# Second-stage scores over all 128 rows of the matmul array, fed by copies of their operands, with the second-stage products moved behind the first stage's

## The chip, the cores and the metric

The kernel runs on one core of a Trainium2 chip. The metric is the device time of one execution in microseconds (us); smaller is better. The engines are named as the profile names them: PE (matmuls; PEld is its weight load), DVE, ACT and POOL (work on rows of elements), SP (here it only issues DMA transfers). Each engine runs its own instructions strictly in the order in which they were built, and waits where an operand or a buffer isn't there yet.

## The reference

Two attentions follow each other. The first has 8 batches of 8 heads over 576 positions of width 64, and keeps only scores within tau of their row's maximum. Its output, heads side by side, is x of the second, which has four experts with causal attention; each row takes the two experts with the highest gate.

```python
scores = scale * np.matmul(q, k.transpose(0, 1, 3, 2))
thresh = np.max(scores, axis=-1, keepdims=True) - tau
scores = np.where(scores >= thresh, scores, -1000000000.0)
attn = softmax(scores); x = heads_side_by_side(np.matmul(attn, v))
...
for e in range(E):                      # E = 4 experts of width 64
    q = x @ wq[e]; k = x @ wk[e]; v = x @ wv[e]
    scores = scale * (q @ k.transpose(0, 2, 1))
    scores = np.where(causal, -1000000000.0, scores)
    ye = softmax(scores) @ v @ wo[e]
    out += (gate weight of e, zero unless e is in the top 2) * ye
```

## The kernel before

**Tiles and stages.** The 576 positions are four row tiles of 128 and a rest of 64 (`R = 4`, tile number 4 is the rest, for both heads at once). Heads are taken in pairs: pair `n` of 32, four pairs to a batch. The main loop has one step per row tile of a pair (`i = 5n + s`, tiles in the order `TS`). A step scores a tile (`scores`: PE into PSUM bank pairs, DVE maximum, ACT exponential, DVE threshold, POOL normalization), transposes the tile of two steps ago (`transp`, PE and ACT), prepares the next pair's q and k (`prep`), and at steps 1 and 4 of a pair multiplies transposed tiles by the values (`attnv`).

**Precision.** Operands of the scores are split into a rounded high part and a rest. In the first stage DMA copies inside SBUF (`spread`, queue of SP) lay high part and rest of q above each other, 64 rows each, so that a head needs two products over 128 rows. In the second stage, before the change, a head needs three products over 64 rows (high times high, high times rest, rest times high: `HHL`); expert 0 of an expert pair lies in rows 0 to 63 and expert 1 in rows 64 to 127, so their products alternate between the two halves of the array.

**The second stage** runs one batch behind the first. For batch `b` and expert pair `ep` (0 or 1), which together are called a key here, there are projections (`project`, PSUM tiles `pj`), values and gates (`values`, `v2`), scores (`scores2`, `s2`, over `w = 128 (t + 1)` columns for row tile `t`, then a causal mask added by a bf16 product), transposes (`transp2`, `t2`), products with the values (`attnv2`, `av2`) and at the end `output` (`o`). In the profile the digit of a name is dropped, so `s2` reads `s`, `t2` reads `t`, `av2<-pt2,v2` reads `av<-pt,v`.

**Order.** A plan in Python writes the program: `pe[1]` is the plan's own clock for PE, `fill` puts second-stage pieces into a step until the step's share is used, `tiled` is called at steps 1 to 4 of a pair and puts in up to two due value products and one score tile, and `AFTER_...` are the waits that the plan leaves between a piece and its follower. `pr` gives every instruction a priority, by which a scheduler then sets each engine's order. Second-stage PSUM tiles come from four banks (`ps_g`) that transposes, projections and value products share; a full score tile takes two of them, one per expert.

**Array shapes.** The profile writes rows*columns of the array in use: 128*128 for most products, 128*64 for products with values (`av`), and 64*128 for the second-stage scores of row tiles 0 to 3.

Of the kernel before, what the change touches and what calls it, by code (L numbers as in the profile page):

```python
# [28 lines left out]
AFTER_S2, AFTER_V, AFTER_T2, AFTER_AV2 = 7000, 8500, 1800, 2000  # L29
BETWEEN_S2, AFTER_V_END = 2000, 5000  # L30

# [7 lines left out]
CUT = 2  # L39
T_END = (2, 3, 4, 1, 0)  # L40
T_MID = (4, 3, 2, 1, 0)
# [7 lines left out]
    "max": -0.509, "thr": -0.091, "exp": 0.327, "stt": -2.461, "sum": -1.419, "nrm": 0.098,  # L49
# [6 lines left out]
PPB = 4  # L56
P2B = 3
PTB = 9
PTTB = 4
VB = 3  # L60
E_PTT = "A"
# [3 lines left out]
def kernel(  # L65
# [112 lines left out]
    def load_pair(n):  # L178
        b, hp = divmod(n, NPAIR)
        hs = slice(2 * hp, 2 * hp + 2)  # L180
        vm = one.tile([P, 2, R, D], F32, tag="vm", name=f"vm_{n}", bufs=VB)
        pr("ld")
        def load(dst, src):
            r = nc.sync.dma_start(dst, src)
            if n in (1, 2):
                tc.add_manual_dep(r.ins, SPREAD[0].name, NOSYNC, reason="order")
        for t, x in ((km, k), (qm, q)):
            load(t[:, :, :R], x[b, hs, :SM, :].rearrange("h (p r) d -> p h r d", r=R))
            load(t[:ST, :, R], x[b, hs, SM:, :].rearrange("h s d -> s h d"))
        load(vm, v[b, hs, :SM, :].rearrange("h (p r) d -> p h r d", r=R))  # L190
        for j, rows in enumerate((slice(0, ST), slice(ST, P))):
            load(vtz[n % VB][rows, j], v[b, 2 * hp + j, SM:, :])
        VS[n] = (vm, vtz[n % VB])

# [246 lines left out]

    q2ds = [zeros(f"q2d{i}") for i in range(2)]
    Q2, V2, GW, GT = {}, {}, {}, {}

    def project(b, ep, cs):

        first, last = cs[0] == 0, cs[-1] == NC - 1
        for i, (wh, wl) in enumerate(((wqh, wql), (wkh, wkl))):
            if last:
                Q2[b, ep, i] = one.tile([P, 2, S], F32R, tag=f"q2{ep}{i}", name=f"q2_{b}_{ep}_{i}")  # L450
            t = Q2.get((b, ep, i))
# [88 lines left out]
    def scores2(b, t, ep):  # L540
        q2, k2 = Q2[b, ep, 0], Q2[b, ep, 1]
        nmx = small.tile([P, 2], F32, tag="nmx", name=f"nm2_{b}_{ep}_{t}")
        sm = small.tile([P, 2], F32, tag="sm", name=f"sm_{b}_{ep}_{t}")
        pr("s2")
        if t < R:
            w = (t + 1) * P
            if b == B - 1:
                g = ps_s.tile([P, 2, 512], F32, tag="s", name=f"s2_{b}_{t}_{ep}")
                gg = [g[:, j] for j in range(2)]
            else:  # L550
                gg = [gbank(f"s2_{b}_{t}_{ep}_{j}") for j in range(2)]
            for i, (x, y) in enumerate(HHL):
                for j in range(2):
                    sl = slice(j * D, (j + 1) * D)
                    matmul(gg[j][:, :w], q2[sl, x, t * P:w], k2[sl, y, :w], start=(i == 0), stop=False)
            for j in range(2):
                matmul(gg[j][:, t * P:w], ident_b, mask, start=False, stop=True)
            views = [g[:, :w] for g in gg]
        else:
            w = S  # L560
            g = ps_s.tile([P, 2, 512], F32, tag="s", name=f"s2_{b}_{t}_{ep}")
            for hf in range(2):
                cols = slice(hf * HS, (hf + 1) * HS)
                for i, (x, y) in enumerate(HHL):
                    matmul(g[:, hf, :HS], q2ds[ep][:, x], k2[:, y, cols],
                                     start=(i == 0), stop=(hf == 0 and i == 2))
# [108 lines left out]
    def project_some():  # L675

        while proj:
            b, what, g = proj[0]
            if what == "v" and left.get(b - 1, 0) or any(x[1] == b - 1 and what == f"q{x[3]}" for x in S2):
                return False  # L680
            try:
# [4 lines left out]
                if what[0] == "q":  # L686
                    S2.extend((0, b, t, int(what[1])) for t in (T_MID if b < B - 1 else T_END))
                elif what == "v":
# [3 lines left out]
        return False  # L692

    def score_tile():
        _, b, t, ep = S2.pop(0)
        scores2(b, t, ep)
        if b in GW and not unscaled:
            scale2(b, t, ep)
# [13 lines left out]
    def transposable():  # L712
        return due(T2) and len(unscaled) < len(T2) and len(A2) < 2

# [18 lines left out]

    def tiled():

        for _ in range(2):
            if due(A2):
                value_tile()
        if S2 and S2[0][2] < R and len(T2) < P2B:
            score_tile()  # L740
# [10 lines left out]
    for _ in prep(0):  # L751
        pass
    load_pair(1)
    pre = iter(())
    goal = 0.0
    for i in range(N + 2):
# [24 lines left out]
        if slot:  # L781
            m, at = (n, 4) if s == 4 else (n - 1, 6)
            if 0 <= m < NPR:
                attnv(m, TS[slice(*AV_AT[at])])
                if at == 6 and m % NPAIR == NPAIR - 1:
                    begin(m // NPAIR)
            tiled()
        else:
            next(tr, None)
            if s in MORE:  # L790
                tiled()
        for _ in sc:
# [8 lines left out]
        fill(goal)  # L801
        if S2 and S2[0][2] == R and len(T2) < P2B:
            score_tile()
# [3 lines left out]
    while proj or S2 or T2 or A2 or O2:  # L807
# [7 lines left out]
        elif transposable():  # L815
            transpose_tile()
        elif S2 and len(T2) < (P2B if S2[0][1] < B - 1 else PPB) and pe[1] >= since:
            score_tile()
# [33 lines left out]
```

## Time and profile before

| | |
|---|---|
| device time, median of 3 runs | 1035.93 us (1033.07 to 1035.97) |
| profiled execution: own time | 1033.38 us |
| profiled execution: span from first to last instruction | 1031.7 us |
| PE, DVE, ACT, POOL busy, share of the span | 94%, 79%, 63%, 40% |
| granted PE clock, mean | 0.99 |

The span is 1.7 us shorter than the execution's own time. A busy share counts the modelled time of instructions. In a timeline, the distance from the start of one matmul to the start of the next is what a matmul costs PE in a dense stream; the duration beside it is its whole passage and overlaps with the next.

### The profile page before, as it was taken

What the parts mean: (1) busy time and instruction counts of PE and PEld (TensorE: products, weight loads), DVE (VectorE), ACT (ScalarE), POOL (GpSimd) and SP (SyncE); (2) the same over time, 40 slices, a digit from 0 to 9 for tenths busy, and PEclk for the clock granted to TensorE, in tenths of its full rate; (3) what the DMA queues carried; (4) which work ended last, traced back from release to release, by engine and by line L of the source; (5) the groups of instructions that cost most, each with busy time, mean ns of one, the idle gap of its engine ahead of it and who ended that gap; (6) DMA issues with size and microseconds to landing.
All of it is one profiled execution on the core that took longest, in us unless ns stands there. A gap on an engine that the chain in (4) does not pass through costs nothing.

```text
span 1031.7 us, 26572 instructions
## 1 busy us (share of the span) xinstructions
PE 966.5 (94%) x9520; PEld 863.5 (84%) x9520; DVE 816.5 (79%) x2374; ACT 651.6 (63%) x1564; POOL 408.4 (40%) x700
## 2 busy tenths in 40 slices
PE   4778999999999999999999999999999999999998
PEld 3676898789888898888987898978988889888975
DVE  4778688877888779888789878887788877988564
ACT  3667566765667656765667656676566765676554
POOL 2556424533244334443344332453324533433122
PEclk9998999999999999999999999999999999999999
DMA  6555423344223443225343242334322344311101
GB/s 156 142 128 141 121 73 91 102 117 119 59 72 95 133 112 93 61 68 143 90 103 94 72 124 75 91 102 126 110 56 73 96 132 112 79 30 44 42 2 46
DMA packets 83891, 96.11 MB, mean 93 GB/s; under 512 B 29745, under 2 KB 54321, under 8 KB 83761
## 3 DMA queue, kind: packets, MB, share of 16 engines
q1 hardware_dynamic: 83296, 93.83, 34.5%
q8 instruction: 76, 1.25, 0.5%
q10 hardware_dynamic: 464, 0.59, 0.2%
q14 instruction: 55, 0.44, 0.1%
HBM read 30.42 MB, written 9.44 MB: 39 GB/s over the span
## 4 chain that ended last, share of the span: by engine, by line
PE 59%; DVE 17%; ACT 13%; issue 5%; POOL 4%; DMA 1%; SPq 0%; DVEq 0%; ACTq 0%; POOLq 0%
PE av L159 18%; PE s L159 13%; PE tm L162 8%; PE pj L159 7%; DVE pp L356 5%; PE v L159 4%; PE o L159 4%; ACT p L575 3%; ACT pp L354 3%; PE t L162 3%; DVE nmx L349 3%; DVE x L439 2%; ACT pt L144 2%; PE qkT L162 2%; POOL pp L364 2%
## 5 line engine op out<-in xcount | busy, mean ns | idle before, releaser
L364 POOL TENSOR_SCALAR pp<-pp,ss 128x576 f32<-128x576 f32 x288 | 212.8, 750 | 408.4 <-DVE ss L370 313.0
L356 DVE SCALAR_TENSOR_TENSOR pp<-s,thr,pp 128x576 f32<-128x576 f32 x288 | 233.0, 814 | 77.3 <-ACT pp L354 72.5
L354 ACT ACTIVATE pp<-s,nmx 128x576 f32<-128x576 f32 x288 | 213.7, 746 | 80.6 <-DVE nmx L349 76.8
L349 DVE TENSOR_REDUCE nmx<-s 128x1 f32<-128x576 f32 x288 | 215.8, 751 | 41.6 <-PE s L159 40.4
L159 PE MATMUL s<-kt,qt 128*128 128x288 f32 x1024 | 205.3, 319 | 5.8 <-DMA qt<-hl 5.4
L162 PE MATMUL tm<-ident,pp 128*128 128x128 f32 x1152 | 166.2, 278 | 22.1 <-POOL pp L364 15.8
L159 PE MATMUL av<-pt,vm 128*64 128x128 f32 (+1 forms) x2560 | 167.8, 267 | 0.0
L159 PEld LDWEIGHTS s<-kt,qt 128*128 128x128 f32 x1024 | 151.9, 194 | 15.5 <-DMA qt<-hl 5.7
L162 PEld LDWEIGHTS tm<-ident,pp 128*128 128x128 f32 x1152 | 136.1, 143 | 33.2 <-POOL pp L364 22.6
L159 PEld LDWEIGHTS av<-pt,vm 128*64 128x64 f32 x2560 | 140.0, 138 | 15.4 <-issue 11.4
L144 ACT COPY pt<-tm 128x512 f32<-128x512 f32 x199 | 113.6, 589 | 58.6 <-PE tm L162 56.3
L575 ACT ACTIVATE p<-s,nm 128x384 f32<-128x384 f32 (+3 forms) x144 | 78.9, 551 | 63.4 <-DVE nm L573 59.0
L589 POOL TENSOR_SCALAR p<-p,sm,gw 128x512 f32<-128x512 f32 (+3 forms) x128 | 77.1, 610 | 81.4 <-ACT pt L144 35.4
L140 ACT ACTIVATE x<-av 128x256 fp32r<-128x256 f32 (+1 forms) x96 | 48.0, 500 | 71.5 <-PE av L159 49.6
L573 DVE TENSOR_REDUCE nm<-s 128x1 f32<-128x384 f32 (+3 forms) x144 | 71.1, 513 | 24.2 <-PE s L159 21.4
L162 PE MATMUL t<-ident,p 128*128 128x128 f32 x384 | 61.1, 284 | 15.9 <-DVE ss L369 8.9
L159 PE MATMUL av<-ptt,vtz 128*64 128x128 f32 (+1 forms) x640 | 68.8, 263 | 0.0
L140 ACT ACTIVATE pt<-t 128x512 f32<-128x512 f32 (+2 forms) x112 | 57.9, 541 | 15.6 <-PE t L162 14.2
L159 PE MATMUL v<-wvh,x 128*128 128x260 f32 x320 | 64.8, 287 | 0.0
L162 PEld LDWEIGHTS t<-ident,p 128*128 128x128 f32 x384 | 43.0, 144 | 25.9 <-POOL p L589 14.3
L439 DVE TENSOR_TENSOR x<-av,x 128x256 fp32r<-128x256 f32 (+1 forms) x96 | 47.6, 495 | 19.2 <-ACT x L140 16.0
L159 PE MATMUL av<-pt,v 128*64 128x128 f32 (+1 forms) x896 | 57.9, 262 | 1.9 <-ACT p L575 1.2
(132 smaller groups left out, 1808.9 us busy)
## 6 DMA issues: line engine op xcount, KB each, us to landing
kt<-hl SPq DMA_DIRECT2D x252, 144.0 KB, 2.7
qt<-hl SPq DMA_DIRECT2D x128, 128.0 KB, 2.4
km<-in_k_dram SPq DMA_DIRECT2D x32, 256.0 KB, 3.0
qm<-in_q_dram SPq DMA_DIRECT2D x32, 256.0 KB, 3.2
vm<-in_v_dram SPq DMA_DIRECT2D x32, 256.0 KB, 2.8
out_dram<-ob SPq DMA_DIRECT2D x32, 256.0 KB, 2.4
km<-in_k_dram SPq DMA_DIRECT2D x32, 32.0 KB, 2.7
qm<-in_q_dram SPq DMA_DIRECT2D x32, 32.0 KB, 2.7
```

The source lines that it names most:

```text
L140: nc.scalar.activation(dst, src, AF.Copy)
L144: nc.any.tensor_copy(dst, src)
L159: queued(nc.tensor.matmul(out, x, y, **kw), x, ns if x.shape[0] == P else ns / 2)
L162: queued(nc.tensor.transpose(out, x, ident), x, 109)
L349: nc.vector.tensor_reduce(nmx[:, js], sv, axis=AX.XY, op=ALU.max, negate=True)
L354: nc.scalar.activation(e, sv, AF.Exp, bias=nmx[:, js])
L356: nc.vector.scalar_tensor_tensor(e, sv, thr[:, js], e, op0=ALU.is_ge, op1=ALU.mult, accum_out=ss[:, js])
L364: nc.gpsimd.tensor_scalar(p, p, ss[:, h:h + 1], 0.0, op0=ALU.mult, op1=ALU.add)
L439: nc.vector.tensor_tensor(xl, gs, xh.bitcast(F32), op=ALU.subtract)
L573: nc.vector.tensor_reduce(nmx[:, j:j + 1], sv, axis=AX.X if t < R else AX.XY, op=ALU.max, negate=True)
L575: nc.scalar.activation(p2[:, j * SM:j * SM + w] if t < R else halves(p2[:, :S]), sv, AF.Exp, bias=nmx[:, j:j + 1], accum_out=sm[:, j:j + 1])
L589: nc.gpsimd.tensor_scalar(p, p, sm[:, j:j + 1], gg[:, j:j + 1], op0=ALU.mult, op1=ALU.mult)
```

## The change

It has four parts. The second-stage score operands are copied into two new tiles (`q2x`, `k2x`) by twelve DMA copies on SP's queue per key (`spread2`), as the first stage does it, and an expert's scores are two products over 128 rows in place of three over 64; the row tile of the rest stays as it was. Score tiles of up to 256 columns hold both experts in one PSUM bank. Due value products of the second stage are put in only at steps 1 and 4, directly behind the first stage's (up to three), and no longer at steps 2 and 3; up to three transposed tiles may wait for them, where it was two. Buffers follow: one pair of `q2` tiles for both expert pairs where there were two, two value buffers (`VB`) where there were three, their loads behind `attnv`, and for the last batch the order `T_END` begins with tile 4.

```diff
-BETWEEN_S2, AFTER_V_END = 2000, 5000
+BETWEEN_S2, AFTER_V_END, AFTER_SPREAD = 2000, 5000, 6000
-T_END = (2, 3, 4, 1, 0)
+T_END = (4, 2, 3, 1, 0)
-VB = 3
+VB = 2
...
+    def spread2(b, ep):
+        qs, ks = Q2[b, ep, 0], Q2[b, ep, 1]
+        heads = [slice(j * D, (j + 1) * D) for j in range(2)]
+        q2x, k2x = X2 if (b, ep) != (B - 1, EP - 1) else (
+            two.tile([P, 2, SM], F32R, tag="qt", name="q2x_end"),
+            two.tile([P, 2, 2, S], F32R, tag="kt", name="k2x_end")[:, :, :, :SM])
+        Q2[b, ep] = (q2x, k2x)
+        pr("dm2")
+        for j, sl in enumerate(heads):
+            for x, rows in enumerate(heads):
+                for dst, src in ((q2x[rows, j], qs[sl, x, :SM]), (k2x[heads[0], j, x], ks[sl, x, :SM]),
+                                 (k2x[heads[1], j, x], ks[sl, x, :SM])):
+                    nc.sync.dma_start(dst.bitcast(F32), src.bitcast(F32))
...
-                gg = [gbank(f"s2_{b}_{t}_{ep}_{j}") for j in range(2)]
-            for i, (x, y) in enumerate(HHL):
-                for j in range(2):
-                    sl = slice(j * D, (j + 1) * D)
-                    matmul(gg[j][:, :w], q2[sl, x, t * P:w], k2[sl, y, :w], start=(i == 0), stop=False)
+                g = gbank(f"s2_{b}_{t}_{ep}_0")
+                gg = [g, g[:, w:] if 2 * w <= 512 else gbank(f"s2_{b}_{t}_{ep}_1")]
             for j in range(2):
+                for i in range(2):
+                    matmul(gg[j][:, :w], q2x[:, j, t * P:w], k2x[:, j, i, :w], start=(i == 0), stop=False)
                 matmul(gg[j][:, t * P:w], ident_b, mask, start=False, stop=True)
...
-        return due(T2) and len(unscaled) < len(T2) and len(A2) < 2
+        return due(T2) and len(unscaled) < len(T2) and len(A2) < 3
...
-    def tiled():
-        for _ in range(2):
+    def tiled(most):
+        for _ in range(most):
             if due(A2):
                 value_tile()
-        if S2 and S2[0][2] < R and len(T2) < P2B:
+        if scorable(False) and len(T2) < P2B:
             score_tile()
...
-            tiled()
+            tiled(3)
         else:
             next(tr, None)
             if s in MORE:
-                tiled()
+                tiled(0)
```

The built order shows three places. The first is a score tile of 256 columns on PE, in the second stage of batch 3 (`s2_3_1_1` is row tile 1 of its expert pair 1), with the row ahead of it; before:

```order
L159 MATMUL av2_3_4_1_8700<-pt2t_3_1_8610,v2_3_7530 64x64 x2
L159 MATMUL s2_3_1_1_0_8715<-q2_3_1_1_8035,q2_3_1_0_7970 128x256 x3
L159 MATMUL s2_3_1_1_1_8716<-q2_3_1_1_8035,q2_3_1_0_7970 128x256 x3
L159 LDWEIGHTS ident_b_78
L159 MATMUL s2_3_1_1_0_8715<-mask_80,ident_b_78 128x128
L159 LDWEIGHTS ident_b_78
L159 MATMUL s2_3_1_1_1_8716<-mask_80,ident_b_78 128x128
L159 MATMUL s_19_4_0_8746<-hl_19_8279,qd1_116 128x288 x6
```

Now, the same score tile:

```order
L159 MATMUL s_19_1_1_8863<-kt_19_8190,qt_19_8189 128x288 x3
L159 MATMUL s2_3_1_1_0_8924<-k2x_123,q2x_122 128x256 x2
L159 LDWEIGHTS ident_b_78
L159 MATMUL s2_3_1_1_0_8924<-mask_80,ident_b_78 128x128
L159 MATMUL s2_3_1_1_0_8924<-k2x_123,q2x_122 128x256 x2
L159 LDWEIGHTS ident_b_78
L159 MATMUL s2_3_1_1_0_8924<-mask_80,ident_b_78 128x128
L162 MATMUL t2_3_3_1_0_8940<-ident_73,p2_3_3_1_8671 128x128 x4
```

Six products into two PSUM tiles became four into one, each expert's mask follows its own products, and the rows ahead of it and behind it now use the whole array, as it does itself.

The second place is a value product of the same batch on PE (`av2_3_1_0`); before it stands alone at a step 3, between transposes and a score tile:

```order
L162 MATMUL tm_18_0_1_8560<-ident_73,pp_18_0_8298 128x128 x4
L162 MATMUL tt_18_0_8567<-ident_73,pp_18_0_8298 128x128
L159 MATMUL av2_3_1_0_8573<-pt2_3_1_0_0_8449,v2_3_7530 64x128 x4
L159 MATMUL s2_3_2_1_0_8582<-q2_3_1_1_8035,q2_3_1_0_7970 128x384 x3
L159 MATMUL s2_3_2_1_1_8583<-q2_3_1_1_8035,q2_3_1_0_7970 128x384 x3
```

Now value products stand behind the first stage's, and the next score tile behind them (`av_18_2` is the first stage's):

```order
L159 MATMUL av_18_2_8792<-ptt_18_3_8760,vtz0_100 64x128 x2
L159 MATMUL av2_3_0_0_8821<-pt2_3_0_0_0_8728,v2_3_7670 64x128 x2
L159 MATMUL av2_3_4_1_8826<-pt2_3_4_1_0_8774,v2_3_7670 64x64 x8
L159 MATMUL av2_3_4_1_8826<-pt2t_3_1_8778,v2_3_7670 64x64 x2
L159 MATMUL s2_3_2_1_0_8841<-k2x_123,q2x_122 128x384 x2
```

Rows of one array shape were moved together: over the whole program PE's order before changes its array shape 328 times from one matmul to the next, and 192 times now.

The third place is SP's queue where the copies of batch 3's expert pair 1 fall, behind the last copies for pair 19; before:

```order
L282 DMA qt_19_8280<-hl_19_8279 64x512 x4
L184 DMA km_97<-in_k_dram 64x2x64
L184 DMA qm_96<-in_q_dram 128x2x256
L184 DMA qm_96<-in_q_dram 64x2x64
L657 DMA out_0_dram<-ob_3_4_8779 64x512
```

Now:

```order
L290 DMA qt_19_8189<-hl_19_8188 64x512 x4
L468 DMA q2x_122<-q2_3_1_0_8077 64x512
L468 DMA k2x_123<-q2_3_1_1_8342 64x512 x2
L468 DMA q2x_122<-q2_3_1_0_8077 64x512
L468 DMA k2x_123<-q2_3_1_1_8342 64x512 x2
L468 DMA q2x_122<-q2_3_1_0_8077 64x512
L468 DMA k2x_123<-q2_3_1_1_8342 64x512 x2
L468 DMA q2x_122<-q2_3_1_0_8077 64x512
L468 DMA k2x_123<-q2_3_1_1_8342 64x512 x2
L183 DMA km_97<-in_k_dram 64x2x64
L183 DMA qm_96<-in_q_dram 128x2x256
```

Twelve copies stand ahead of the loads for the next pair; the first six serve expert 0, the other six expert 1, and the first of each six waits for PE's last product from the tiles that it overwrites.

## Rows read from the trace of the kernel before

**Rows 1.** The page: busy time of PE and DVE, and the chain by engine.

```profile
PE 966.5 (94%) x9520; PEld 863.5 (84%) x9520; DVE 816.5 (79%) x2374; ACT 651.6 (63%) x1564; POOL 408.4 (40%) x700
...
PE 59%; DVE 17%; ACT 13%; issue 5%; POOL 4%; DMA 1%; SPq 0%; DVEq 0%; ACTq 0%; POOLq 0%
```

**Rows 2.** Windows (length, busy PE, PEld, DVE, ACT, POOL): one batch; the end.

```profile
477.80:600.20 122.40, 118.50 (x1192) 106.56 (x1191) 101.21 (x296) 79.50 (x192) 48.66 (x80) 1.00 0.37 96
...
976.50:1031.70 55.20, 48.14 (x410) 38.42 (x404) 29.38 (x96) 26.60 (x80) 13.51 (x24) 0.97 0.07 25
```

**Rows 3.** Timeline of PE (start, duration in us): a shape kept, a shape changed.

```profile
490.60 0.27 PE L162 MATMUL tt<-ident,pp 128*128 128x128 f32 x1
490.71 0.27 PE L162 MATMUL qkTt<-ident,qi 128*128 128x128 f32 x1
...
503.91 0.27 PE L162 MATMUL tt<-ident,pp 128*128 128x128 f32 x1
504.11 0.45 PE L159 MATMUL av<-pt,vm 128*64 128x64 f32 x6
```

**Rows 4.** Timeline of PE: score tiles of the four widths that run without a stop.

```profile
508.00 0.96 PE L159 MATMUL s<-q,q 64*128 64x512 f32 x6
508.90 0.28 PE L159 MATMUL s<-mask,ident_b 128*128 128x128 bf16 x2
508.99 0.38 PE L159 MATMUL s<-hl,qd 128*128 128x288 f32 x1
...
517.46 0.79 PE L159 MATMUL s<-q,q 64*128 64x384 f32 x6
518.18 0.28 PE L159 MATMUL s<-mask,ident_b 128*128 128x128 bf16 x2
...
994.91 0.63 PE L159 MATMUL s<-q,q 64*128 64x256 f32 x6
995.47 0.28 PE L159 MATMUL s<-mask,ident_b 128*128 128x128 bf16 x2
...
548.92 0.55 PE L159 MATMUL s<-q,q 64*128 64x128 f32 x6
549.40 0.28 PE L159 MATMUL s<-mask,ident_b 128*128 128x128 bf16 x2
```

**Rows 5.** Timeline of PE: products over all 128 rows, 512 and 288 columns.

```profile
479.84 0.39 PE L159 MATMUL o<-wol,zh 128*128 128x512 f32 x1
...
480.77 0.40 PE L159 MATMUL o<-woh,zl 128*128 128x512 f32 x1
...
488.05 0.69 PE L159 MATMUL s<-kt,qt 128*128 128x288 f32 x4
488.58 0.43 PE L159 MATMUL pj<-x,wqh 128*128 128x288 f32 x2
```

**Rows 6.** Timeline of PE: score tiles that stop on the way.

```profile
560.94 1.21 PE L159 MATMUL s<-q,q 64*128 64x384 f32 x6
562.08 0.29 PE L159 MATMUL s<-mask,ident_b 128*128 128x128 bf16 x2
...
569.47 0.62 PE L159 MATMUL s<-q,q 64*128 64x256 f32 x3
570.34 0.61 PE L159 MATMUL s<-q,q 64*128 64x256 f32 x3 [0.26 <-DVE zl L642]
570.89 0.28 PE L159 MATMUL s<-mask,ident_b 128*128 128x128 bf16 x2
```

**Rows 7.** DMA issues (size, us to landing), and the timeline of SP's queue.

```profile
kt<-hl SPq DMA_DIRECT2D x252, 144.0 KB, 2.7
...
526.51 3.69 SPq L282 DMA_DIRECT2D kt<-hl  x6
```

**Rows 8.** Timeline of PE: two stops at the end of the program.

```profile
997.92 3.18 PE L162 MATMUL t<-ident,p 128*128 128x128 f32 x14 [2.17 <-POOL p L589]
...
1014.64 1.41 PE L162 MATMUL t<-ident,p 128*128 128x128 f32 x8 [0.76 <-POOL p L589]
```

More of the change, by code (lines that the diff above doesn't have):

```diff
@@ L180, in load_pair @@
         hs = slice(2 * hp, 2 * hp + 2)
-        vm = one.tile([P, 2, R, D], F32, tag="vm", name=f"vm_{n}", bufs=VB)
         pr("ld")
@@ L189, in load_pair, with load_values, load @@
             load(t[:ST, :, R], x[b, hs, SM:, :].rearrange("h s d -> s h d"))
-        load(vm, v[b, hs, :SM, :].rearrange("h (p r) d -> p h r d", r=R))
+    def load_values(n):
+        b, hp = divmod(n, NPAIR)
+        vm = one.tile([P, 2, R, D], F32, tag="vm", name=f"vm_{n}", bufs=VB)
+        pr("ld")
+        def load(dst, src):
+            r = nc.sync.dma_start(dst, src)
+            if n < 2:
+                tc.add_manual_dep(r.ins, SPREAD[0].name, NOSYNC, reason="order")
+        load(vm, v[b, 2 * hp:2 * hp + 2, :SM, :].rearrange("h (p r) d -> p h r d", r=R))
         for j, rows in enumerate((slice(0, ST), slice(ST, P))):
@@ L442 @@
     q2ds = [zeros(f"q2d{i}") for i in range(2)]
+    X2 = (const.tile([P, 2, SM], F32R, name="q2x"), const.tile([P, 2, 2, SM], F32R, name="k2x"))
     Q2, V2, GW, GT = {}, {}, {}, {}
+    def spread2(b, ep):
[11 more added lines that the diff above has]
+                    nc.sync.dma_start(dst.bitcast(F32), src.bitcast(F32))
     def project(b, ep, cs):
@@ L449, in project @@
             if last:
-                Q2[b, ep, i] = one.tile([P, 2, S], F32R, tag=f"q2{ep}{i}", name=f"q2_{b}_{ep}_{i}")
+                Q2[b, ep, i] = one.tile([P, 2, S], F32R, tag=f"q2{i}", name=f"q2_{b}_{ep}_{i}")
             t = Q2.get((b, ep, i))
@@ L540, in scores2 @@
     def scores2(b, t, ep):
-        q2, k2 = Q2[b, ep, 0], Q2[b, ep, 1]
         nmx = small.tile([P, 2], F32, tag="nmx", name=f"nm2_{b}_{ep}_{t}")
@@ L545, in scores2 @@
         if t < R:
+            q2x, k2x = Q2[b, ep]
             w = (t + 1) * P
@@ L564, in scores2 @@
                 for i, (x, y) in enumerate(HHL):
-                    matmul(g[:, hf, :HS], q2ds[ep][:, x], k2[:, y, cols],
+                    matmul(g[:, hf, :HS], q2ds[ep][:, x], Q2[b, ep, 1][:, y, cols],
                                      start=(i == 0), stop=(hf == 0 and i == 2))
@@ L678, in project_some @@
             b, what, g = proj[0]
-            if what == "v" and left.get(b - 1, 0) or any(x[1] == b - 1 and what == f"q{x[3]}" for x in S2):
+            if what == "v" and left.get(b - 1, 0) or what[0] == "q" and any(x[2] == R or (x[1], x[3]) != spread[0] for x in S2):
                 return False
@@ L687, in project_some @@
                     S2.extend((0, b, t, int(what[1])) for t in (T_MID if b < B - 1 else T_END))
+                    spread_next()
                 elif what == "v":
@@ L692, in project_some, with spread_next, scorable @@
         return False
+    spread = [None, 0.0]
+    def spread_next():
+        if S2:
+            key = (S2[0][1], S2[0][3])
+            if key != spread[0]:
+                spread2(*key)
+                spread[:] = key, pe[1] + AFTER_SPREAD
+    def scorable(tail):
+        return S2 and (S2[0][2] == R) == tail and (tail or pe[1] >= spread[1])
     def score_tile():
@@ L696, in score_tile @@
         scores2(b, t, ep)
+        spread_next()
         if b in GW and not unscaled:
@@ L753 @@
     load_pair(1)
+    load_values(0)
     pre = iter(())
@@ L784 @@
                 attnv(m, TS[slice(*AV_AT[at])])
+            if s == 1 and n + 1 < NPR:
+                load_values(n + 1)
+            if 0 <= m < NPR:
                 if at == 6 and m % NPAIR == NPAIR - 1:
                     begin(m // NPAIR)
-            tiled()
+            tiled(3)
         else:
@@ L801 @@
         fill(goal)
-        if S2 and S2[0][2] == R and len(T2) < P2B:
+        if scorable(True) and len(T2) < P2B:
             score_tile()
@@ L816 @@
             transpose_tile()
-        elif S2 and len(T2) < (P2B if S2[0][1] < B - 1 else PPB) and pe[1] >= since:
+        elif S2 and scorable(S2[0][2] == R) and len(T2) < (P2B if S2[0][1] < B - 1 else PPB) and pe[1] >= since:
             score_tile()
```

2 rows, old and new, of the table PR are left out of this document.

## The prediction

> **What bounds the kernel now.** I read the page first: PE is busy 94% of the span, DVE, the next, 79%, and the chain that ended last lies 59% on PE [rows 1]. A mean over unlike stages can mislead, so I then asked for windows of one batch's length. From the second batch on they repeat: in 122.4 us PE is busy 118.5, DVE 101.2, ACT 79.5, POOL 48.7 [rows 2]. So in seven eighths of the span PE has 3.9 us of idle time per batch and no other engine less than 21. Only the end, after the first stage, is loose: 48.1 busy of 55.2 us [rows 2], with two stops in which transposes wait for POOL's scaled rows, 2.17 and 0.76 us [rows 8]. What PE is spared in the batches should therefore come off the time, as long as no engine that feeds it is later than now.
>
> A busy time doesn't say what a matmul costs, since matmuls overlap. I price PE by the distance from one start to the next.
>
> **1. Fewer changes of array shape (gain).** A transpose followed by one of its own shape takes 0.11 us to the next start (490.60 to 490.71), followed by a product of another shape 0.20 (503.91 to 504.11) [rows 3]. A change of shape costs 0.09 us. The built order has 328 of them before and 192 now: 64 half-height score tiles no longer enter and leave a shape of their own, and value products stand behind the first stage's. 136 x 0.09 = 12.2 us less. This is work of PE alone, so nothing hides it.
>
> **2. Two full-height products for three half-height ones (loss).** From the first product of a score tile to its first mask, the clean tiles take 0.90, 0.72, 0.56 and 0.48 us for 512, 384, 256 and 128 columns [rows 4]. The step to the mask holds a change of shape, counted above; without it 0.81, 0.63, 0.47 and 0.39, together 2.30. Now each tile has four products over all rows. Four of 512 columns take 0.93 us (479.84 to 480.77), four of 288 take 0.53 (488.05 to 488.58) [rows 5]; between the two lie 0.70 for 384. For 128 columns I take the transpose's 0.11 each, 0.44; for 256, between 0.44 and 0.53, 0.48. Together 2.55. With 16 keys the loss is 16 x 0.25 = 4.0 us. The bounds: the prices at 128 and 256 columns could each be as low as proportional to columns (0.23 and 0.47, loss 0.5 us) or as high as that of 288 (0.53 both, loss 6.2); I keep 4.0, since the transpose is the nearest row. Two masks in a row take 0.09 us (508.90 to 508.99) [rows 4], and standing apart they should cost the same: nothing.
>
> The Trainium skill speaks against this part: "TensorEngine Tiling (Array Packing)", section "Theoretical Speedup", gives a contraction of at most 64 rows up to twice the speed, two half-height products at a time. By that rule six would cost three full ones, 1.91 us over the four widths, the change would lose 16 x 0.64 = 10.2 us in place of 4.0, and the sum below would end near 1030. The trace has 2.30, so the pairs reach the rule only in part (0.81 us against 0.70 at 512 columns).
>
> **3. Stops inside score tiles (gain).** In expert pair 1 the tile of 256 columns takes 1.42 us to its mask (569.47 to 570.89) and the one of 384 takes 1.14 (560.94 to 562.08) [rows 6], where clean ones take 0.56 and 0.72 [rows 4]. In the first, the second expert's products wait until DVE has emptied their PSUM bank (0.26 us shown as idle at 570.34), and three products of one expert in a row find no partner in the other half. A tile of up to 256 columns now takes one bank, and no halves are left: that stop should go, 0.86 x 7 batches = 6.0 us. At 384 two banks are still taken, and I count nothing of its 0.42 x 7 = 2.9. Bounds: 0 (the stop moves to the next taker of a bank) to 8.9.
>
> **4. Twelve copies per key on SP (hidden, barely).** Copies of this size leave SP 0.62 us apart (3.69 us for 6) and land after 2.7 [rows 7]. Expert 0's first product needs four of them: 3 x 0.62 + 2.7 = 4.6 us after they may start; expert 1's last needs all: 11 x 0.62 + 2.7 = 9.5. For expert pair 0 the order leaves about 15 us of PE work between the projection and the first score. For pair 1 the tiles must first be given up by pair 0's last scores. Between these and pair 1's first product, PE's order in batch 3 has 9 transposes and 38 value products of 128 columns (0.11 each, the latter priced like a transpose), 10 narrow value products (0.06), 18 score products of 288 columns (0.13) and 4 changes of shape: 1.0 + 4.2 + 0.6 + 2.3 + 0.4 = 8.5 us, and some 10 before expert 1's. So the copies are covered, the last ones by half a microsecond. Behind them SP holds the loads of the next pair's k and q; what waits on those is the next transposes of k, whose copies are needed only at the next pair. In the first two batches copies for the next pair's keys stand between the twelve; there I charge 1 us at two keys, 2 us.
>
> **5. The end (loss).** Expert pair 0's first score tile of the last batch waits for its copies, and the transposes of that tile now follow 1.7 us of PE work after its scores, where before no tile had less than 4.5 (both summed along the order by the prices above). I charge a second pair of stops like those shown, 2.17 + 0.76 = 2.9 us [rows 8]; bounds 0 and 6.
>
> The moved value loads and the smaller `VB` cost nothing: the tile is loaded right after its last reader at step 1 of a pair, and is needed at step 4 of the second pair after it, over 30 us later against a landing of 2.7 [rows 7]. Holding three transposed tiles takes some of the nine `pt` buffers longer; along the order, in three of eight batches one copy out of PSUM meets a buffer whose reader is about 4 us of PE work away; ACT's and the banks' slack should cover most of it.
>
> **The sum.** -12.2 + 4.0 - 6.0 + 2.0 + 2.9 = -9.3 us. The profiled execution took 1033.4 us itself, 1.7 more than its span; it lies at the lower end of the runs shown, 2.5 below their median. 1033.4 - 9.3 = 1024.1; for a median of runs I put **1025 us**. With the bounds of each term, my forecast's own range is 1014 to 1031.
>
> **Rivals.** (A) *The copies come late.* If SP reaches the twelve late, or they land late, PE stands at pair 1's first scores with everything queued behind them: the first stage's scores and transposes, and so DVE, ACT and POOL. Each microsecond of lateness at 8 such keys costs 8 us. At 1.2 us the gain is gone, beyond 1.6 the kernel is slower by more than the measurement hides; at 3 us it takes 1024 + 24 = 1048. For it: a cover of only half a microsecond for the last copies, and pair 19's own `qt` copies directly ahead of them. Against: `kt` and `qt`, copied in the same way, keep PE waiting nowhere in the batches shown, and PE's real pace is slower than the bare prices (118.5 busy us in a batch), which gives the copies more time. The page "DMA: Bandwidth & Descriptors" of the Trainium skill, section "Rules for kernel authors", advises against splitting a transfer into two partition halves, since both use the same engines; here the halves come from different rows, and no row of this trace shows one whole copy beside them.
>
> (B) *The freed time isn't passed on.* PE's gain per batch, about 1.2 us, is small beside the chain's 30% on DVE and ACT [rows 1]; if PE merely waits longer for normalized rows, the time stays at 1031 to 1037. Against it: PE's 3.9 idle us per batch, with 21 spare on DVE [rows 2].
>
> (C) *More stops go* than I count (the 384 tile's, no new ones at the end): 1024.1 - 2.9 - 4.9, about 1016, lowest 1012.
>
> **How the numbers follow.** My forecast has 0.64, C 0.08, B 0.14, A 0.14. What this kernel's runs can tell from no change is about 0.3%, 3 us: faster is below 1032.8. My forecast and C are faster throughout; of B nearly all is the same; of A a sixth or so lands within, the rest is slower. That makes faster 0.73, same 0.15, slower 0.12. A range of 1013 to 1037 keeps my forecast, most of C, all of B and the mildest of A, some 0.85.
>
> **What would show it.** Right: PE has no 64*128 row, and a window of a steady batch is 121 us or shorter; four products of a 512-wide tile take about 0.93 us, of a 128-wide one 0.44; the 256-wide tile of pair 1 passes without a stop. Wrong: waits of PE for a DMA into `q2x` or `k2x` (A), or for POOL at transposes growing by a microsecond per batch (B); the prediction fails too if a change of shape costs less where the order now bunches products than where I read it, or if the end grows by more than 6 us.

## The result, and the profile after

The changed kernel takes 1021.19 us (median of 4 runs, 1019.25 to 1021.56); the kernel before took 1035.68 beside it (1033.07 to 1035.97). The ratio is 0.986, 95% interval 0.984 to 0.988: faster by 14.5 us, less than 2% but clear of the noise, where the prediction had 1025 and a range of 1013 to 1037. The profiled execution has a span of 1019.5 us.

The page of the changed kernel, busy times and chain, answers to [rows 1]:

```profile
PE 948.5 (93%) x9392; PEld 861.5 (85%) x9392; DVE 819.9 (80%) x2387; ACT 645.8 (63%) x1551; POOL 408.8 (40%) x699
...
PE 66%; DVE 14%; ACT 9%; POOL 4%; issue 4%; DMA 2%; SPq 1%; DVEq 0%; POOLq 0%; ACTq 0%
```

Windows of the changed kernel (from and to, length, busy PE, PEld, DVE, ACT, POOL with instructions, granted PE clock, DMA share, GB/s) answer to [rows 2]: two batches, five batches, the rest of the program from the start of batch 8, and the end.

```profile
349.40:466.70 117.30, 113.81 (x1161) 104.63 (x1159) 101.54 (x295) 76.57 (x184) 49.28 (x80) 1.00 0.50 127
466.70:589.10 122.40, 116.83 (x1192) 107.43 (x1191) 100.66 (x297) 80.96 (x199) 48.25 (x81) 1.00 0.47 122
...
228.00:828.80 600.80, 576.67 (x5856) 529.18 (x5856) 507.22 (x1481) 392.96 (x951) 243.82 (x401) 1.00 0.49 125
828.80:1019.50 190.70, 180.65 (x1681) 161.43 (x1679) 136.40 (x403) 108.41 (x283) 59.48 (x97) 0.97 0.34 87
...
960.00:1019.50 59.50, 51.45 (x377) 42.10 (x375) 30.17 (x97) 25.55 (x79) 13.05 (x22) 0.90 0.31 83
```

The kernel before, over the same five batches (third to seventh, each from its first score product) and the rest:

```profile
233.00:845.50 612.50, 592.74 (x5952) 532.79 (x5951) 505.83 (x1472) 397.58 (x960) 243.35 (x400) 1.00 0.36 96
845.50:1031.70 186.20, 175.25 (x1679) 154.34 (x1677) 134.49 (x397) 108.77 (x280) 59.48 (x97) 0.99 0.19 51
```

Five batches are 11.7 us shorter: PE is busy 16.1 us less, and 4.4 of that come back as idle time (19.8 before, 24.1 now). The batches no longer read alike: one takes 117.3, the next 122.4, as all did before. The rest of the program is 4.5 us longer, at a lower granted clock. Both losses turn out to come with the copies (below).

### The profile page after: what moved, and what is told of

Read it like the earlier page. It is cut to its first block, busy times and chain, and to the rows that moved or that the text cites. A ratio compares the mean times of both kernels' runs of the same rounds, so it can differ in the third digit from the quotient of the medians.

```text
span 1019.5 us, 26681 instructions
## 1 busy us (share of the span) xinstructions
PE 948.5 (93%) x9392; PEld 861.5 (85%) x9392; DVE 819.9 (80%) x2387; ACT 645.8 (63%) x1551; POOL 408.8 (40%) x699
## 4 chain that ended last, share of the span: by engine, by line
PE 66%; DVE 14%; ACT 9%; POOL 4%; issue 4%; DMA 2%; SPq 1%; DVEq 0%; POOLq 0%; ACTq 0%
PE av L159 19%; PE s L159 17%; PE tm L162 8%; PE pj L159 7%; PE o L159 5%; DVE nmx L357 4%; PE v L159 4%; DVE pp L364 3%; ACT pp L362 3%; PE t L162 3%; POOL pp L372 2%; PE qkT L162 2%; ACT p L600 2%; DVE x L447 1%; ACT x L140 1%
## 5 line engine op out<-in xcount | busy, mean ns | idle before, releaser
L364 DVE SCALAR_TENSOR_TENSOR pp<-s,thr,pp 128x576 f32<-128x576 f32 x288 | 233.0, 814 | 59.5 <-ACT pp L362 50.6
L159 PE MATMUL av<-pt,vm 128*64 128x128 f32 (+1 forms) x2560 | 164.7, 267 | 0.5 <-ACT pt L144 0.5
L159 PEld LDWEIGHTS av<-pt,vm 128*64 128x64 f32 x2560 | 137.4, 138 | 15.0 <-issue 7.9
L144 ACT COPY pt<-tm 128x512 f32<-128x512 f32 x186 | 106.7, 591 | 59.7 <-PE tm L162 58.9
L600 ACT ACTIVATE p<-s,nm 128x256 f32<-128x256 f32 (+4 forms) x144 | 79.4, 554 | 46.8 <-DVE nm L598 46.1
L598 DVE TENSOR_REDUCE nm<-s 128x1 f32<-128x256 f32 (+4 forms) x144 | 72.2, 514 | 18.4 <-PE s L159 14.6
L159 PE MATMUL s<-k2x,q2x 128*128 128x384 f32 (+3 forms) x240 | 62.9, 362 | 9.6 <-ACT p L600 3.6
L159 PE MATMUL av<-ptt,vtz 128*64 128x128 f32 (+1 forms) x640 | 66.3, 263 | 0.0
L162 PE MATMUL t<-ident,p 128*128 128x128 f32 x384 | 59.5, 284 | 5.3 <-POOL p L614 2.1
L359 DVE SCALAR_TENSOR_TENSOR thr<-nmx,tau_p 128x1 f32<-128x1 f32 x288 | 54.0, 193 | 2.2
```

Of the source, the lines that this page charges most:

```text
L144: nc.any.tensor_copy(dst, src)
L159: queued(nc.tensor.matmul(out, x, y, **kw), x, ns if x.shape[0] == P else ns / 2)
L162: queued(nc.tensor.transpose(out, x, ident), x, 109)
L364: nc.vector.scalar_tensor_tensor(e, sv, thr[:, js], e, op0=ALU.is_ge, op1=ALU.mult, accum_out=ss[:, js])
L598: nc.vector.tensor_reduce(nmx[:, j:j + 1], sv, axis=AX.X if t < R else AX.XY, op=ALU.max, negate=True)
L600: nc.scalar.activation(p2[:, j * SM:j * SM + w] if t < R else halves(p2[:, :S]), sv, AF.Exp, bias=nmx[:, j:j + 1], accum_out=sm[:, j:j + 1])
```

## The experiments

Each time is a median of 4 to 6 runs, beside runs of the kernel before on the same chip (medians 1033.4 to 1034.0 there, 1.7 to 2.2 us below the 1035.7 of the result; so runs are best compared with the changed kernel by their ratios, its own being 0.984 to 0.988). "Five batches" is the stretch that the windows above show, "rest" what follows it.

| run | us (lowest to highest) | ratio to before, 95% | five batches | rest |
|---|---|---|---|---|
| e1 score part only | 1022.9 (1019.9 to 1026.0) | 0.988 to 0.992 | 598.6 | 192.0 |
| e2 moved products only | 1025.9 (1020.2 to 1029.7) | 0.989 to 0.994 | 598.2 | 190.1 |
| e3 two banks | 1018.0 (1017.4 to 1020.0) | 0.983 to 0.987 | 596.8 | 188.6 |
| e4 no copies | 1004.5 (1003.0 to 1006.6) | 0.970 to 0.974 | 588.8 | 184.3 |
| e5 copies unread | 1001.9 (1000.7 to 1004.4) | 0.966 to 0.971 | 588.5 | 184.7 |
| e6 9000 | 1015.0 (1012.6 to 1017.5) | 0.979 to 0.984 | 591.0 | 191.0 |
| e7 copies twice | 1114.2 (1110.7 to 1117.3) | 1.074 to 1.080 | 656.0 | 210.2 |
| e8 early q0 | 1019.4 (1017.8 to 1022.9) | 0.983 to 0.988 | 600.6 | 188.1 |
| e9 score part only, 9000 | 1012.7 (1012.1 to 1013.2) | 0.978 to 0.982 | 589.6 | 190.6 |
| e10 9000, two banks | 1015.7 (1014.4 to 1017.7) | 0.981 to 0.985 | 595.0 | 188.6 |
| e11 9000, early q0 | 1012.8 (1010.9 to 1013.8) | 0.978 to 0.982 | 590.8 | 189.2 |
| e12 9000, both | 1016.2 (1013.6 to 1019.3) | 0.981 to 0.986 | 595.0 | 187.8 |

**One part alone.** e1 is the changed kernel with the value products left at steps 1 to 4:

```diff
-        return due(T2) and len(unscaled) < len(T2) and len(A2) < 3
+        return due(T2) and len(unscaled) < len(T2) and len(A2) < 2
...
-            tiled(3)
+            tiled(2)
...
-                tiled(0)
+                tiled(2)
```

e2 is the kernel before with the value products moved:

```diff
-        return due(T2) and len(unscaled) < len(T2) and len(A2) < 2
+        return due(T2) and len(unscaled) < len(T2) and len(A2) < 3
...
-    def tiled():
+    def tiled(most):
-        for _ in range(2):
+        for _ in range(most):
...
-            tiled()
+            tiled(3)
...
-                tiled()
+                tiled(0)
```

> The change without the moved value products: they stand at steps 1 to 4 again, at most two at a step, and two transposed tiles may wait. The order has 224 changes of array shape, 32 more than the changed kernel, 104 fewer than before. My theory (the scores over all rows are what pays, through fewer shape changes and the stop that is gone; the moved products pay by shape changes alone): 32 x 0.09 = 2.9 us more than the changed kernel, about 1024 us (1022 to 1027). Rival (the moved products are what pays, since PE then gets score tiles and transposes at quieter places): close to before, 1030 to 1036.

> The kernel before with the value products moved to steps 1 and 4, up to three at a step, nothing else. The order has 306 changes of array shape, 22 fewer than before. My theory: 22 x 0.09 = 2.0 us less than before, with the stops inside half-height score tiles as they were: about 1034 us (1031 to 1036). Rival (moving is what pays): 1026 or less.

e1 came as my theory had it, but partly by chance: the copies come late at more of its keys, and with copies in time (e9, below) it equals the changed kernel. e2 came as the rival had it: 22 changes of shape fewer, 2.0 us by the price of [rows 3], brought about 8. Each part alone shortens the five batches by some 14 us, both together by 11.7. So the parts don't add, and changes of shape are not the measure. What e2 removes besides is in the list of waits; before, over the whole program (us in total, times, longest):

```profile
PE t L162 <- DVE ss L369: 8.9, 7, 1.3
...
PE pj L159 <- ACT ptt L140: 4.0, 7, 0.6
```

and in e2:

```profile
PE t L162 <- DVE ss L369: 1.8, 2, 1.3
...
PE pj L159 <- ACT ptt L140: 0.6, 1, 0.6
```

A stop that is there seven times recurs once per batch, and a new order of the pieces can remove it: the changed kernel has 1.3 us left of the first as well, and so has e1.

**One bank or two.**

```diff
-                gg = [g, g[:, w:] if 2 * w <= 512 else gbank(f"s2_{b}_{t}_{ep}_1")]
+                gg = [g, gbank(f"s2_{b}_{t}_{ep}_1")]
```

> The changed kernel, with the narrow score tiles (128 and 256 columns) in two PSUM banks again, one for each expert. My theory (the stop in the 256-wide tile of pair 1 came from the wait for a second bank): it comes back, 0.86 x 7 = 6.0 us, about 1027 us (1024 to 1030). Rival (the stop came from half-height products that find no partner, and there are none left): no change, 1021 us (1020 to 1022.5).

e3 is at 1018.0, not 1027; by its ratio it can't be told from the changed kernel. The timeline of PE in e3 shows the 256-wide tile of pair 1 with two banks, dense, and then a 128-wide one that stops:

```profile
575.50 0.40 PE L159 MATMUL s<-k2x,q2x 128*128 128x256 f32 x2
...
575.78 0.48 PE L159 MATMUL s<-k2x,q2x 128*128 128x256 f32 x2
...
342.21 0.42 PE L159 MATMUL s<-k2x,q2x 128*128 128x128 f32 x2
342.46 0.23 PE L159 MATMUL s<-mask,ident_b 128*128 128x128 bf16 x1
343.41 0.44 PE L159 MATMUL s<-k2x,q2x 128*128 128x128 f32 x2 [0.71 <-ACT ptt L140]
```

So the stop at the 256-wide tile did not come back, but a second bank still stops PE: in the five batches of e3 five of the ten 128-wide tiles wait 0.37 to 0.72 us between the two experts, until ACT has copied a transposed tile out of PSUM, which no narrow tile of the changed kernel does. These stops cost no time in total. Whether the stops of [rows 6] belonged to the half-height products or to the second bank is therefore not settled. Whether two banks are 3 us better is open: at 9000 (e10) they are not.

**The copies away, and the copies unread.** In e4 the twelve copies are not made and their tiles hold zeros, set once by POOL:

```diff
-                    nc.sync.dma_start(dst.bitcast(F32), src.bitcast(F32))
```

In e5 they are made, but the score products take a table of weights (`wf`, from `wqh`) for both operands:

```diff
-                    matmul(gg[j][:, :w], q2x[:, j, t * P:w], k2x[:, j, i, :w], start=(i == 0), stop=False)
+                    matmul(gg[j][:, :w], wf[:, t * P:w], wf[:, :w], start=(i == 0), stop=False)
```

> The changed kernel without the twelve copies per key; the tiles they fill are set to zero once, so the second-stage scores of row tiles 0 to 3 are computed from zeros. My theory (the copies are hidden, but for the 2.5 us of waits for them that the trace shows and up to 3 us at the end): 1016 to 1020 us, and the tail of the program no more than 3 us shorter. Rival (192 copies on SP's queue and 25 MB more of traffic delay the loads and the first stage's own copies all through the program): 8 to 15 us faster, 1006 to 1013.

> The changed kernel with all twelve copies per key, which nobody reads: the second-stage score products of row tiles 0 to 3 take a table of weights for both operands, so these scores are left out. SP's queue and the traffic are those of the change; only the waits on and for the copied tiles are gone. Theory of the late copies (what the copies cost is PE's wait at the few keys whose cover is short, 6.8 to 8 us from the start of the copies to the first score at batches 0, 3 and 5's pair 1 and at the end, with what queues behind it on DVE): 1002 to 1008 us, like the run without copies. Rival (the 25 MB more of traffic, or SP's 7.5 us per key, slow the first stage's own transfers): near 1020, like the changed kernel.

My expectation of e4 fell: 17 us less, not 1 to 5. e5 says why: with all the copies on SP's queue and all their traffic it takes 1001.9, and its five batches are as long as e4's. (What e4 takes more lies ahead of them: they start at 229.6 us in e4, at 225.1 in e5.) So neither the queue's time nor 25 MB more of traffic costs anything that shows; that score products read copied operands costs 19 us by the times, 18 by the ratios. e5 also takes away their wait for the projection, and its copies need not wait for readers. PE's order in e5 is nearly that of the changed kernel: 467 of 9392 products stand elsewhere, none by more than 26 places. The list of waits of the changed kernel shows only 2.5 us of this as waits for a DMA:

```profile
PE s L159 <- DVE pp L364: 6.6, 11, 1.2
...
PE s L159 <- DMA q2x<-q: 2.5, 3, 1.4
```

The timeline shows the rest. At pair 1 of batch 3, SP issues the copies from 550.50 to 558.80:

```profile
550.50 0.54 SPq L468 DMA_DIRECT2D q2x<-q  x1
...
557.56 1.24 SPq L468 DMA_DIRECT2D k2x<-q  x2
```

PE, from 6.8 us after their start:

```profile
557.32 0.40 PE L159 MATMUL s<-k2x,q2x 128*128 128x512 f32 x1
...
558.35 0.39 PE L159 MATMUL s<-k2x,q2x 128*128 128x512 f32 x1
...
559.39 0.47 PE L159 MATMUL s<-k2x,q2x 128*128 128x512 f32 x1 [0.58 <-DMA q2x<-q]
...
562.02 0.40 PE L159 MATMUL s<-kt,qt 128*128 128x288 f32 x1 [1.18 <-DVE pp L364]
...
562.54 0.47 PE L159 MATMUL s<-k2x,q2x 128*128 128x512 f32 x1
```

and DVE:

```profile
558.84 0.69 DVE L598 TENSOR_REDUCE nm<-s 128x1 f32<-128x512 f32 x1 [1.45 <-PE s L159]
559.45 1.41 DVE L357 TENSOR_REDUCE nmx<-s 128x1 f32<-128x576 f32 x2
```

Four products that take 1.2 us with their masks when dense are spread over 5.5 us. DVE stands 1.45 us at this tile's maximum with the first stage's maxima queued behind it, so the first stage's thresholding is late, and PE then stands 1.18 us for a bank that DVE has not given back. The wait for the DMA is the smallest piece of what the late copy costs. The built order too has moved the tile's products apart, among the first stage's, and the runs don't separate that from the waits; in e5 this tile is dense.

**The copies earlier, and later.** e6 changes one number:

```diff
-BETWEEN_S2, AFTER_V_END, AFTER_SPREAD = 2000, 5000, 6000
+BETWEEN_S2, AFTER_V_END, AFTER_SPREAD = 2000, 5000, 9000
```

e7 issues each copy twice:

```diff
-                    nc.sync.dma_start(dst.bitcast(F32), src.bitcast(F32))
+                    for _ in range(2):
+                        nc.sync.dma_start(dst.bitcast(F32), src.bitcast(F32))
```

> The changed kernel with AFTER_SPREAD at 9000 in place of 6000: the plan leaves 3 us more between the copies and the first score. By the prices of matmuls, PE's order now has 16.6 us of work ahead of every first score of pair 1 in the steady batches, where the changed kernel has 8.9 at two of them and 11.5 at a third; it has 176 changes of shape (192). Theory of the late copies: the stops at those keys go, about 3 x 4 us, and 16 x 0.09 = 1.4 us of shape changes: 1006 to 1011 us. Rival (traffic or SP's time): 1.4 us less, 1018 to 1021.

> The changed kernel with each copy issued twice in a row, so that the last lands about 7.5 us later than now. Theory of the late copies: expert 0's first product needs copies up to the eighth, about 7 us after the start, which the long covers (15 us) hold and the three short ones (7 us) do not; expert 1's last operand comes some 17.5 us after the start, 1.5 after the time at which PE asks for it at a long cover and 8 to 9 after it at a short one: 3 x 8.5 + 10 x 1.5 + 5 at the end, about 45 us more, 1050 to 1075. Rival (traffic): another 15 to 20 us for another 25 MB, 1035 to 1041. My prediction, by which all is hidden with half a microsecond to spare at each pair-1 key: 8 x 7 = 56 us more.

In e6 first scores come 14.9 us or more after the start of their copies in all five batches, and the tile that was spread over 5.5 us is dense (timeline of PE in e6):

```profile
563.21 0.73 PE L159 MATMUL s<-k2x,q2x 128*128 128x512 f32 x2
...
563.83 0.71 PE L159 MATMUL s<-k2x,q2x 128*128 128x512 f32 x2
...
564.42 0.78 PE L159 MATMUL s<-kt,qt 128*128 128x288 f32 x4
```

and the batches are nearly those of e5 (windows of e6, then of e5):

```profile
228.90:819.90 591.00, 574.81 (x5858) 528.51 (x5856) 505.07 (x1468) 396.49 (x957) 242.21 (x400) 1.00 0.49 126
819.90:1010.90 191.00, 179.57 (x1697) 161.62 (x1694) 136.54 (x401) 111.34 (x291) 59.28 (x98) 0.98 0.33 87
```

```profile
225.10:813.60 588.50, 572.76 (x5856) 528.09 (x5856) 506.80 (x1485) 390.68 (x948) 242.79 (x401) 1.00 0.50 127
813.60:998.30 184.70, 176.64 (x1681) 157.73 (x1679) 135.60 (x403) 107.67 (x282) 59.38 (x97) 1.00 0.35 90
```

So e6 gives back 9.8 of the 12.3 us that the copies cost in the five batches. Its order differs in much more than these keys (5371 of PE's 9392 products stand at another place than in the changed kernel), so e6 alone doesn't show that the lateness was the cause. The single batches do. The five take 121.4, 117.3, 122.4, 117.3 and 122.4 us in the changed kernel, and 117.2, 117.3, 118.5, 117.2 and 118.3 in e5, of which the second and third are (beside those of the changed kernel in the section on the result):

```profile
342.30:459.60 117.30, 113.87 (x1161) 104.71 (x1160) 101.52 (x296) 76.62 (x184) 49.09 (x80) 1.00 0.50 127
459.60:578.10 118.50, 115.82 (x1194) 107.21 (x1192) 101.63 (x300) 79.82 (x197) 48.18 (x82) 1.00 0.49 125
```

Each batch has the same copies and the same traffic. All of the 12.3 us lie in the three batches (1, 3 and 5 of the second stage) in which a 512-wide tile is spread over 4 to 5.6 us, about 4 us in each; the other two are as long as in e5.

The total of e6 gained 6 us (4 to 5 by the ratios), not the 10 to 15 expected: the rest of the program kept its 6 us over e5, where the last batch has no work to put behind the copies, and the time scatters by 5 us. e7 took the direction of the theory, but with twice its size: 93 us more. Its list of waits has 31.6 us of PE's waits for copied tiles, and 30.4 for DVE's thresholding, 6.6 in the changed kernel:

```profile
PE s L159 <- DVE pp L364: 30.4, 19, 3.2
PE s L159 <- DMA k2x<-q: 19.7, 9, 3.2
...
PE s L159 <- DMA q2x<-q: 11.9, 6, 4.2
```

**The score part with copies in time.** e9 is e1 with the number of e6.

> The score part of the change alone (value products at steps 1 to 4, at most two, as in the run with the score part only), with AFTER_SPREAD at 9000, so that no pair-1 key of the steady batches has less than 14.2 us of PE work between the last score of pair 0 and its first one (8.4 in that run at six keys). The order has 216 changes of shape, 40 more than the changed kernel at 9000. Theory (copies in time, the moved products are worth their shape changes and no more): 40 x 0.09 = 3.6 us above that kernel's 1015, about 1018.5 (1016 to 1021), and no batch with waits for q2x. Rival (the moved products free stops of their own, as they do without the score part, 8 us): 1022 or more. Third case (both parts free the same stops): equal to 1015 within 2 us.

It takes 1012.7, with no wait for a copy in its list, and 216 changes of shape against 176 in e6, which takes 1015.0. The third case, nearly (2.3 us below, where the case allowed 2): with the copies in time the moved products bring nothing on top, and 40 changes more do not show as 3.6 us. The five batches of e9:

```profile
230.10:819.70 589.60, 577.73 (x5853) 527.24 (x5852) 497.24 (x1463) 398.82 (x962) 243.28 (x400) 1.00 0.49 126
```

PE is busy 2.9 us more than in e6 and idle 4.3 less (11.9 against 16.2): here more work of PE went with less waiting.

**The end.** e8 and e11 project the last batch's first pair ahead of its values; the second edit keeps the first half of the values from scaling score tiles whose gates don't exist yet. e10 and e12 combine edits shown so far.

```diff
-        proj.append((b, "q0", project(b, 0, cs)))
+        proj.insert(sum(x[1] == "p" for x in proj) if b == B - 1 else len(proj), (b, "q0", project(b, 0, cs)))
...
-                elif what == "v":
+                elif what == "v" and b in GW:
```

> The changed kernel with one piece of the last batch moved: the rest of expert pair 0's projection ahead of the values, so that its copies start some 7 us earlier and the values and outputs lie behind them. Theory (what the end grew by, from 186.2 to 190.7 us, are the stops of score tiles and transposes at 980 to 988 us and the low clock behind them): 4 to 6 us less than the changed kernel, 1015 to 1018. Rival (the end is set by the chain through DVE, ACT and POOL of the last tiles, and PE's stops only move): no change, 1020 to 1022.

> The changed kernel with AFTER_SPREAD at 9000 and the last batch's first projection ahead of its values. Theory (with the batches free of late copies, the end still has 6 us of stops that the runs without waits for copies don't have; earlier copies take back a part): 2 to 4 us below 1015, 1011 to 1013. Rival (the end's stops only move, as when this was tried at 6000, where it brought 2 us at most): 1014 to 1016.

> The changed kernel with AFTER_SPREAD at 9000 and two PSUM banks for the narrow score tiles. Theory (the number of banks of a narrow tile decides nothing, since the stops came from half-height products): as with one bank, 1013 to 1017. Rival (one bank costs: both experts' tiles then come free together and late, which the 3 us between 1021 and 1018 showed): 3 us less, 1010 to 1013.

> The changed kernel with all three: AFTER_SPREAD at 9000, two banks for narrow score tiles, the last batch's first projection ahead of its values. If each is worth what its own run shows and they add: 1015 less 3 less 2, about 1010 (1008 to 1013). If two banks and the end bring nothing here: 1014 to 1016.

e8 can't be told from the changed kernel: 1.8 us less by its time, nothing by its ratio. e11 is where the theory put it, 2.2 us below e6, with ranges that overlap. e10 agrees with its theory, 1015.7, so the number of banks does not decide the total at 9000. e12, at 1016.2, shows that the three don't add. Of the versions that compute all scores, e9 and e11 are the best that were run, both some 21 us below before, and their intervals lie wholly under the changed kernel's.

## Why the prediction was right, and where it was not

The forecast held, 1025 against 1021, and PE was the right engine. But the sum came out by terms that missed in both directions, so the closeness is luck. Of the signs that the prediction named, the 256-wide tile passes without a stop, but a batch of 121 us or shorter came in only two of five, and PE does wait for `q2x`.

**1. Changes of shape (-12.2).** Count and price hold: 192 changes in the trace, and over the whole trace of before a transpose `tt` is followed after a median 0.11 us by its own shape (125 of them) and 0.20 by 128*64 (35). That switching the tiling mode drains the engine stands in the Trainium skill, "TensorEngine Tiling (Array Packing)", section "Key Properties"; the 0.09 us agrees. It was read in one direction only: on the way back from 128*64, the first score product behind the value products takes 0.24 us to the next start (34 of them before), where it takes 0.13 in a run. What failed is "nothing hides it": in e9 40 changes more did not show. And e2, which gained four times what its changes are worth, says that a new order changes more than shapes.

**2. Products over all rows (+4.0, bounds 0.5 to 6.2): mis-sized.** A 512-wide tile of the changed kernel in the timeline of PE, and a 128-wide one:

```profile
504.99 0.73 PE L159 MATMUL s<-k2x,q2x 128*128 128x512 f32 x2
505.56 0.23 PE L159 MATMUL s<-mask,ident_b 128*128 128x128 bf16 x1
505.61 0.71 PE L159 MATMUL s<-k2x,q2x 128*128 128x512 f32 x2
506.16 0.23 PE L159 MATMUL s<-mask,ident_b 128*128 128x128 bf16 x1
506.20 0.77 PE L159 MATMUL s<-kt,qt 128*128 128x288 f32 x4
...
578.34 0.44 PE L159 MATMUL s<-k2x,q2x 128*128 128x128 f32 x2
578.62 0.23 PE L159 MATMUL s<-mask,ident_b 128*128 128x128 bf16 x1
578.66 0.42 PE L159 MATMUL s<-k2x,q2x 128*128 128x128 f32 x2
578.92 0.23 PE L159 MATMUL s<-mask,ident_b 128*128 128x128 bf16 x1
578.99 0.82 PE L162 MATMUL t<-ident,p 128*128 128x128 f32 x6
```

The second product of an expert reaches the mask in 0.24 us at 512 columns (median over the trace), as predicted. But two products reach their mask after 0.57 and 0.55, not 0.47, since the first product of each expert is slower: 0.34 us to the next start where it follows value products, 0.31 where it follows a mask, against the 0.23 that [rows 5] show in a run of like products. So masks that stand apart are not free: the one in the middle makes the second expert's first product slow. From the first product to behind the last mask, the undisturbed tiles have medians of 1.21, 0.98, 0.75 and 0.64, together 3.58; the clean ones of [rows 4] have 2.66 to the first mask and 0.09 for two masks each, 3.02, of which 0.36 are changes of shape counted in step 1. The loss is 16 x 0.92 = 14.7 us. By the rule of the Trainium skill that the prediction weighed ("TensorEngine Tiling (Array Packing)", "Theoretical Speedup") it was to be 10.2; that is nearer, but not by that rule: the half-height products are as read, and what was missed is the slow first products and, at 256 columns, a price that was too low.

**3. Stops inside score tiles (-6.0): right that they go, the cause not settled.** e3 has two banks again and no stop at 256 columns, but stops at 128, so it doesn't clear the second bank. And they were larger: before, the four widths have means of 1.03, 1.03, 1.17 and 0.59 us over the five batches, together 3.82, 0.80 more than clean, which would be 12.8 us if all 16 keys were like these ten.

**4. Copies (+2.0): the step that failed.** "So the copies are covered, the last ones by half a microsecond" was read at pair 1 of batch 3 and charged to all alike, and it lets the copies start when pair 0's last scores end. PE gave that key more than was counted, 9.9 us from those scores to the first product where the sum has 8.5. But SP was still issuing pair 19's `qt` copies, and the first of the twelve went out 3.1 us behind pair 0's last score product (PE and SP's queue):

```profile
547.03 0.42 PE L159 MATMUL s<-k2x,q2x 128*128 128x128 f32 x2
...
547.94 2.46 SPq L290 DMA_DIRECT2D qt<-hl  x4
550.50 0.54 SPq L468 DMA_DIRECT2D q2x<-q  x1
```

Rival A had named just these `qt` copies. The trace has short covers there and at two more pair-1 keys, 6.5 to 7.1 us from the first copy to the first score, and 13.9 or more at all others outside the last batch. Where the cover was short it was not enough. Nor was it at the two keys of batch 1, with 16.4 and 13.9 us: there copies for the next pairs stand between the twelve, as the prediction saw, and issuing them took 17.4 and 14.5 us. It charged 2 us for that, and this batch alone is 4.2 longer than in e5. In all, the copied operands cost 18 to 19 us, by e5. So rival A was at work all along; and its price, one microsecond for each of lateness, was too low, since DVE hands the wait on to the first stage.

**5. The end (+2.9): 4.5, within its bounds.** The stops of the changed kernel are 980.48 and 985.69 us in the timeline of PE, and the clock falls behind them:

```profile
980.48 1.06 PE L162 MATMUL t<-ident,p 128*128 128x128 f32 x4 [1.76 <-POOL p L614]
...
981.97 0.77 PE L159 MATMUL s<-k2x,q2x 128*128 128x512 f32 x1
982.54 0.33 PE L159 MATMUL s<-mask,ident_b 128*128 128x128 bf16 x1
...
985.69 0.50 PE L159 MATMUL s<-k2x,q2x 128*128 128x256 f32 x2 [1.56 <-ACT p L600]
```

One 512-wide product takes 0.57 us to the mask behind it there, where it takes 0.24 at a granted clock of 1.00. The end has a mean granted clock of 0.90 over 59.5 us where it was 0.97 over 55.2 [rows 2]: as an estimate, 59.5 x 0.10 = 6.0 us lost to it against 55.2 x 0.03 = 1.7. That difference is about the growth; no run separates the clock from the stops ahead of it.

**What balanced it.** Steps 1 to 3 as now measured are -12.2 + 14.7 - 12.8 = -10 us; without waits for copies the change brought 32 (e5). Some 20 us of gain stand in no term. Part of them are the once-per-batch stops that e2 removes too; by the distances from one start to the next, the largest fall in five batches is behind the first stage's own score products, from 132.8 us (761 of them) to 124.8 (760). In e5 PE's idle time in the five batches is only 4.1 us below before (15.7 against 19.8), its busy time 20.0 below, so most of the unseen gain is not in listed waits. Which piece of the order made it was not settled. So the forecast was near because an unseen gain of some 20 us met a cost of 18 to 19 that was priced at 2.

Rival B, freed time not passed on, held only in small: 4.4 of 16 us in five batches. Rival C's time was not reached by the changed kernel, but e6, e9 and e11 have it.

## What to carry to other kernels

A wait of half a microsecond in the list stood for four us of a batch here: look at what is queued behind the waiting instruction on the next engine, and measure the cost by a run in which the copies are made and nobody waits for them. The cover of a transfer has to be read at every place where it recurs, since the shortest decides, and from the time at which the queue is free to issue it; a planner's margin is then one number to raise. And when two parts of a change remove the same stops, neither's gain may be added to the other's: run each alone.

## What the runs showed of the hardware

Twenty-five MB more of copies inside SBUF on one queue, 121 in place of 96 MB, slowed nothing that could be measured (five batches of 588.5 us in e5 beside 588.8 in e4). The first product behind rows of another kind was slower to the next start than one in a run: the first stage's 288-wide products 0.13 us in a run and 0.22 behind a transpose, though the array shape is the same, in the kernel before. Behind transposes nothing was lost by it, since the product started 0.03 us behind the last transpose where the next transpose takes 0.11. In the stretch from 987.0 to 994.2 us of the changed kernel the granted clock was 0.53, which is the lower of the two levels, 1.2 GHz, for nearly all of it, after PE had been busy 0.13 us in the 1.6 ahead of 985.6 and 0.94 in the next 1.4; in e5, whose end has no waits for copies, it was 1.00 from 970.0 to 997.3 of 998.3 us.
